# Attention and a gated two-matrix layer on one core: five warm-up products, a gate written over its own input in PSUM, its low part of two chunks by minus the identity, offsets in the planned order of the first chunks, and the weight checks moved to the last part

## The chip, the cores and the metric

The kernel runs on one core of one Trainium2 chip. The metric is device time in microseconds (us); lower is better. Engines are named as in the profile: PE (TensorE matmul), PEld (its weight loads), DVE (VectorE), ACT (ScalarE), POOL (GpSimd) and SP (SyncE, which issues the transfers).

## The reference

Attention with a causal window of 128 keys and 4 sink keys over q, k, v of [4, 8, 768, 64]; its output, as x of [3072, 512], goes through two matrices with a gate between them:

```python
keep = is_sink | in_window
scores = np.where(keep, scores, -1000000000.0)
a = np.exp(scores - np.max(scores, axis=-1, keepdims=True))
a = a / (np.sum(a, axis=-1, keepdims=True) + 1e-09)
x = (a @ v) ... reshape(3072, 512)
h = x @ w_in            # w_in [512, 2048]
g = h * np.cos(h)
return (g @ w_out).astype(np.float32)   # w_out [2048, 512]
```

## The kernel before

The 3072 rows are 12 chunks of 256 rows (two row blocks of 128). Chunks 0 to 2 are the first 256 rows of three batches. A chunk passes through 8 slots; a slot is 256 of the 2048 inner columns, so there are 96 slots, numbered 0 to 95.

**One slot**, built by `dense` (L562). Float32 accuracy comes from splitting every factor into a rounded high part and the rest, with three products for each product.
- `h_mm` (L399): 24 products of 256 columns on PE into the PSUM tile `h`, of one bank.
- `turns` (L408, ACT) writes `yt` from `h`; `rest` (L414, DVE) writes `r` in SBUF from `h` and `yt`; `cosine` (L421, ACT) works on `r` in place.
- `gate` (L426, DVE) multiplies `h` by `r` into `r`. With it `h` has been read for the last time and its bank is free.
- `g_hi` (L432, ACT) rounds `r` to `ghi`; `g_lo` (L438, DVE or POOL) writes `glo` = `r` - `ghi`.
- `out_mm` (L447): 12 products of 512 columns on PE from `ghi`, `glo` and w_out into `acc`, one PSUM bank for each row block.

Two `ghi` and two `glo` tiles exist (`GHI`, `GLO`), so `ghi` of slot m waits for the last product of slot m-2. The banks of `h` rotate: two for chunks 0 and 1, three from chunk 2 on; `h` of slot m+3 there takes the bank of slot m. After slot 7 of a chunk `out_copy` (L388) brings `acc` into a raw buffer and `out_store` (L463, SP) stores it.

**Weights** arrive as 32 pieces of 512 KB with two words a value. `load` (L492, SP) fills one of two raw buffers, three DVE instructions (L500, L506, L512) put the value together in `wt`, `round_hi` (L533, ACT) makes the high part and `rest_lo` (L536, DVE or POOL) the low part. All 32 go through chunk 0's time. **Checks**: `check_piece` (L543) loads each piece once more into a raw buffer (L556, SP), and DVE reduces it to one column of `tiny` (L551). At the end `tiny` is reduced to `tmin` (L1250, DVE), turned by one product (L1252, PE), reduced (L1253) and compared (L1254) into `redo`, which each engine loads (L1383) to branch (L1384) over the general path. The raw buffers are shared by weights, checks and output copies.

**The order of the work** on every engine is fixed while the kernel is built: `Plan.order` takes steps by a priority (a planned time) as their inputs come ready in its model, with the constants in `C`. One check goes to each slot from chunk 2 on (`if a > 1`), so the checks fill chunks 2 to 5, and the reduction L1250 is reached in chunk 6. `FILL` is a number of idle products (L1195) that PE may take early; `WARM` is the number of products (L251) ahead of the product `both` (L270), from which DVE gets the mask's limits (`neg` L275, masks L277 to L285).

## Time and profile before

| | us |
|---|---|
| median of 3 runs | 776.79 (775.74 to 777.22) |
| the profiled execution | 777.87 |
| its span, first to last instruction | 776.1 |
| busy: PE, DVE, ACT, POOL | 753.7, 611.7, 575.2, 151.5 |
| mean granted TensorE clock | 0.990 |

The sum of a forecast is made against the profiled execution, 777.87, and then set against the median, 1.08 lower. PE is busy for 97% of the span, so a change is read from what PE waits for, stretch by stretch, and from what stands ahead of the first and behind the last product. The stretches used below run from one chunk's output stores to the next.

### The profile page before, as it was taken

How to read it: one execution, taken by the hardware profiler on the slowest of the kernel's cores; microseconds unless marked ns; L12 is line 12 of the kernel's file. 1: busy time of each engine (PE TensorE's matmuls, PEld its weight loads, DVE VectorE, ACT ScalarE, POOL GpSimd, SP SyncE). 2: the span in 40 equal slices, each digit the busy share in tenths (PEclk: the TensorE clock that was granted, in tenths of full speed). 3: DMA queues.
4: the chain of work that ended last, by engine and by line, in shares of the span. 5: the costliest groups of instructions: out<-in, count | busy, mean ns of one | idle time of the engine just before them, and what ended most of it. 6: DMA issues, size and time to landing. Idle time of an engine off the chain costs nothing.

```text
span 776.1 us, 15387 instructions
## 1 busy us (share of the span) xinstructions
PE 753.7 (97%) x5029; PEld 666.3 (86%) x5029; DVE 611.7 (79%) x1607; ACT 575.2 (74%) x1337; POOL 151.5 (20%) x233
## 2 busy tenths in 40 slices
PE   8999879999999999999999999999999999999996
PEld 7677658888988999888989999999999999999994
DVE  6778878877878988989879988888878987964432
ACT  2768685779887787787886887897798788784332
POOL 1112101120313432122224221210211221220000
PEclk9999989999999999999999999999999999999998
DMA  5564464423265375375366352232242233110000
GB/s 157 142 177 131 142 175 143 109 56 53 47 179 121 57 185 138 67 190 140 64 158 177 58 114 53 43 74 41 40 87 51 50 71 61 30 40 3 28 1 32
DMA packets 215390, 71.51 MB, mean 92 GB/s; under 512 B 204036, under 2 KB 204036, under 8 KB 215300
## 3 DMA queue, kind: packets, MB, share of 16 engines
q1 hardware_dynamic: 215300, 70.43, 38.2%
q8 instruction: 42, 0.69, 0.4%
q14 instruction: 48, 0.39, 0.2%
HBM read 64.09 MB, written 6.29 MB: 91 GB/s over the span
## 4 chain that ended last, share of the span: by engine, by line
PE 79%; DVE 9%; DMA 5%; ACT 3%; issue 2%; SPq 1%; POOL 0%; DVEq 0%; ACTq 0%; POOLq 0%
PE h L399 30%; PE acc L447 29%; PE av L967 4%; PE tp L913 4%; PE s L811 4%; PE s L755 3%; PE av L943 2%; DMA raw<-in_moe_w_in_dram 2%; PE idle L1195 2%; DMA xk<-in_k_dram 1%; DVE glo L438 1%; DVE wt L551 1%; DVE plo L929 1%; DVE r L414 1%; DVE p L824 1%
## 5 line engine op out<-in xcount | busy, mean ns | idle before, releaser
L399 PE MATMUL h<-xhi,whi_in 128*128 128x256 f32 x768 | 223.3, 291 | 0.2 <-DVE r L426 0.2
L399 PE MATMUL h<-xlo,whi_in 128*128 128x256 f32 x768 | 217.0, 283 | 0.0
L399 PE MATMUL h<-xhi,wlo_in 128*128 128x256 f32 x768 | 216.7, 282 | 0.0
L447 PE MATMUL acc<-whi_out,ghi 128*128 128x512 f32 x384 | 158.0, 411 | 3.6 <-ACT whi_out L533 3.6
L399 PEld LDWEIGHTS h<-xhi,whi_in 128*128 128x128 f32 x768 | 145.6, 190 | 12.3 <-issue 2.7
L399 PEld LDWEIGHTS h<-xhi,wlo_in 128*128 128x128 f32 x768 | 145.9, 190 | 7.6
L447 PE MATMUL acc<-wlo_out,ghi 128*128 128x512 f32 x384 | 152.3, 397 | 0.0
L447 PE MATMUL acc<-whi_out,glo 128*128 128x512 f32 x384 | 151.5, 395 | 0.0
L399 PEld LDWEIGHTS h<-xlo,whi_in 128*128 128x128 f32 x768 | 145.8, 190 | 0.1
L824 DVE CUSTOM_DVE_ANT_0 p<-s,mk 128x264 f32<-128x264 f32 (+1 forms) x192 | 76.9, 401 | 35.1 <-PE s L811 22.6
L833 ACT ACTIVATE p<-p,st 128x264 f32<-128x264 f32 (+1 forms) x192 | 93.4, 488 | 0.7
L421 ACT ACTIVATE r<-r,neg 128x512 f32<-128x512 f32 x96 | 69.0, 724 | 27.5 <-DVE r L414 25.2
L447 PEld LDWEIGHTS acc<-whi_out,glo 128*128 128x128 f32 x384 | 72.6, 189 | 16.7
L432 ACT CAST ghi<-r 128x512 fp32r<-128x512 f32 x96 | 59.1, 616 | 31.8 <-PE acc L447 30.8
L438 DVE TENSOR_TENSOR glo<-r,ghi 128x512 fp32r<-128x512 f32 x80 | 57.2, 715 | 30.3 <-ACT ghi L432 29.6
L447 PEld LDWEIGHTS acc<-whi_out,ghi 128*128 128x128 f32 x384 | 73.1, 190 | 8.9 <-ACT whi_out L533 3.9
L447 PEld LDWEIGHTS acc<-wlo_out,ghi 128*128 128x128 f32 x384 | 73.4, 191 | 4.4 <-DVE wlo_out L536 0.4
L426 DVE TENSOR_TENSOR r<-h,r 128x512 f32<-128x512 f32 x96 | 65.3, 682 | 10.6 <-ACT r L421 10.2
L414 DVE SCALAR_TENSOR_TENSOR r<-h,yt 128x512 f32<-128x512 f32 x96 | 65.6, 683 | 6.1 <-ACT yt L408 3.7
L408 ACT ACTIVATE yt<-h 128x512 int32<-128x512 f32 x96 | 57.2, 596 | 14.9 <-PE h L399 13.0
L866 POOL TENSOR_TENSOR vr<-v,vr 128x192 fp32r<-128x192 f32 (+1 forms) x59 | 35.0, 593 | 159.1 <-ACT vr L861 140.9
L811 PE MATMUL s<-r,l 128*128 128x264 f32 (+2 forms) x288 | 61.0, 291 | 3.2 <-DVE r L802 1.7
(132 smaller groups left out, 1382.7 us busy)
## 6 DMA issues: line engine op xcount, KB each, us to landing
raw<-in_moe_w_in_dram SPq DMA_DIRECT2D x32, 512.0 KB
raw<-in_moe_w_out_dram SPq DMA_DIRECT2D x32, 512.0 KB
xk<-in_k_dram SPq DMA_DIRECT2D x256, 48.0 KB
out_dram<-raw SPq DMA_DIRECT2D x24, 256.0 KB
v<-in_v_dram SPq DMA_DIRECT2D x64, 96.0 KB
xq<-in_q_dram SPq DMA_DIRECT2D x144, 32.0 KB
v<-in_v_dram SPq DMA_DIRECT2D x32, 64.0 KB
xq<-in_q_dram SPq DMA_DIRECT2D x24, 64.0 KB
```

Source lines behind the costliest of these rows:

```text
L399: nc.tensor.matmul(out=o.h[:, t, :], lhsT=w[:, c, fs], rhs=xx[:, c, :], start=(c == 0 and n == 0), stop=(c == NC - 1 and n == 2),)
L408: nc.scalar.activation(out=yt, in_=o.h, func=AF.Copy, scale=INV2PI, bias=0.25)
L414: nc.vector.scalar_tensor_tensor(out=o.r, in0=o.h, scalar=INV2PI, in1=yt, op0=ALU.mult, op1=ALU.subtract)
L421: nc.scalar.activation(out=o.r, in_=o.r, func=AF.Sin, scale=TWOPI_DOWN, bias=quarter)
L426: nc.vector.tensor_tensor(out=o.r, in0=o.h, in1=o.r, op=ALU.mult)
L432: nc.scalar.copy(out=o.ghi, in_=o.r)
L438: e.tensor_tensor(out=o.glo, in0=o.r, in1=f32(o.ghi), op=ALU.subtract)
L447: nc.tensor.matmul(out=x.acc[j], lhsT=gg[:, t, j * P : (j + 1) * P], rhs=w[:, f, :], start=(f == 0 and n == 0), stop=(f == NFT - 1 and n = ...
L811: nc.tensor.matmul(out=o.s_ps[j][:, :w], lhsT=o.l[:, j * P : (j + 1) * P], rhs=r.rearrange("p n s -> p (n s)")[:, c0 : c0 + w], start=(n = ...
L824: nc.vector.tensor_tensor_reduce(out=o.p[:, j, :w], in0=o.s_ps[j][:, :w], in1=masks[min(o.i0 + j, 2)][:, :w], op0=ALU.add, op1=ALU.min, sc ...
L833: nc.scalar.activation(out=o.p[:, j, :w], in_=o.p[:, j, :w], func=AF.Exp, bias=o.lead.st[:, 0, o.nth, j : j + 1], scale=-1.0, accum_out=o. ...
L866: e.tensor_tensor(out=o.vr[:, :, 1, :], in0=o.v32, in1=f32(o.vr)[:, :, 0, :], op=ALU.subtract)
```

## The change

`WARM` goes from 11 to 5 and `FILL` from 100 to 68. The gate is written over `h` in PSUM. `ghi` is rounded from `h`, and `glo` is `h` - `ghi`, on DVE alone. In chunks 0 and 1 (`GM` = 2, 16 slots) a product of minus the identity with `ghi` adds -`ghi` to `h`, and ACT or DVE copies the rest to `glo`. `h` is now freed by `glo` and no longer by the gate, and it is begun and ended as one accumulation for the bank. The other constants of `C` are retuned, and `FIRST` holds offsets to the planned times of chunks 0 to 2. Checks are spread by a rule on the slots left: 19 stand in chunks 6 to 10 and 13 in the last chunk.

```diff
 C = {
-    ... "FILL": 100, ... "WARM": 11, ...
+    ... "CR": 1.618, "CS": 0.48, ... "FILL": 68, ... "GM": 2, ... "WARM": 5, ...
 }
+FIRST = {
+    "A": [7.43, 0.93, 2.38], "H": [0.45, -15.92, 4.04], "L": [-4.97, 5.1, 45.76], "M": [1.52, 2.74, 2.39],
+    "Q": [-7.6, -1.04, 10.09], "S": [-1.48, 6.81, 1.33], "V": [15.27, 1.57, 8.4], "W": [0.0, 0.59, 1.67],
+    "X": [12.35, 1.06, -9.48],
+}
...
-                        start=(c == 0 and n == 0), stop=(c == NC - 1 and n == 2),
+                        start=(t == 0 and c == 0 and n == 0), stop=(t == FG - 1 and c == NC - 1 and n == 2), skip_group_check=True,
...
-            nc.vector.tensor_tensor(out=o.r, in0=o.h, in1=o.r, op=ALU.mult)
+            nc.vector.tensor_tensor(out=o.h, in0=o.h, in1=o.r, op=ALU.mult)
...
-            nc.scalar.copy(out=o.ghi, in_=o.r)
+            nc.scalar.copy(out=o.ghi, in_=o.h)
...
-            e.tensor_tensor(out=o.glo, in0=o.r, in1=f32(o.ghi), op=ALU.subtract)
+            e.tensor_tensor(out=o.glo, in0=o.h, in1=f32(o.ghi), op=ALU.subtract)
+    def g_minus(o):
+        def fn(e):
+            nc.tensor.matmul(out=o.h, lhsT=minus, rhs=o.ghi, start=False, stop=True, skip_group_check=True)
+    def g_rest(o):
+        def fn(e):
+            o.glo = mp.tile([P, FG, NT], F32R, name=f"glo_{o.m}", tag="glo", bufs=C["GLO"])
+            copy(e, o.glo, o.h)
...
-            bh.users += [a0, a2, a4]
-            a6 = add(sub(FG * NT), g_lo(o), [a5, blo], t + C["DM"] + 10.8, port=True)
+            users = [a0, a2, a4, a5]
+            if plan.minus and a < C["GM"]:
+                m = add([("PE", 0.23)], g_minus(o), [a5], tm + 10.5)
+                c = [("ACT", act(FG * NT, False)), ("DVE", dve(FG * NT))]
+                a6 = add(c, g_rest(o), [m, blo], tm + 10.8)
+                users.append(m)
+            else:
+                a6 = add([("DVE", dve(FG * NT))], g_lo(o), [a5, blo], tm + 10.8)
+            bh.users += users + [a6]
...
-            if a > 1 and len(checked) < len(checks):
+            left = len(slots) - nh
+            while len(checked) < len(checks) - C["CR"] * min(left, NSLOT) - C["CS"] * max(left - NSLOT, 0):
                 checked.append(check_piece(plan, t + C["CK"], len(checked), checks[len(checked)][2]))
```

Three places show what that does to the order. **SP, its last transfers** (`raw` are the two raw buffers, `out_dram` the output). Before:

```order
L463 DMA out_dram<-raw_70 128x512
L704 DMA v_0_76<-in_v_dram 128x3x64
L463 DMA out_dram<-raw_71 128x512
L704 DMA v_1_77<-in_v_dram 128x3x64
L463 DMA out_dram<-raw_70 128x512
L463 DMA out_dram<-raw_71 128x512
L463 DMA out_dram<-raw_70 128x512
L463 DMA out_dram<-raw_71 128x512
```

With the change:

```order
L485 DMA out_dram<-raw_71 128x512
L485 DMA out_dram<-raw_70 128x512
L578 DMA raw_71<-in_moe_w_out_dram 128x1024
L578 DMA raw_70<-in_moe_w_out_dram 128x1024
...
L485 DMA out_dram<-raw_71 128x512
L485 DMA out_dram<-raw_70 128x512
L578 DMA raw_71<-in_moe_w_out_dram 128x1024
L1414 UNCONDITIONAL_BRANCH x2
L1417 TENSOR_LOAD redo
```

Twelve loads of checks (two are shown) now stand between the stores of chunk 10 and those of the last chunk, and a 32nd stands behind the last store, in the buffer that the first of the two stores reads.

**DVE, its last instructions** (slots 94 and 95; `L573 ISA` are the checks, each with a second instruction that writes its column). Before:

```order
L414 SCALAR_TENSOR_TENSOR r_95_9993<-h_95_9938,yt_81 128x512
L426 TENSOR_TENSOR r_95_9993<-h_95_9938,r_95_9993 128x512
L438 TENSOR_TENSOR glo_94_10011<-r_94_9951,ghi_94_10006 128x512
L438 TENSOR_TENSOR glo_95_10027<-r_95_9993,ghi_95_10022 128x512
L1253 TENSOR_REDUCE tmin_10052<-tp_10054 1x1
L1254 TENSOR_SCALAR redo_89<-tmin_10052 1x1
```

With the change:

```order
L437 TENSOR_TENSOR h_95_9909<-h_95_9909,r_95_9967 128x512
L449 TENSOR_TENSOR glo_94_9985<-h_94_9858,ghi_94_9978 128x512
L573 ISA wt1_73,tiny_88<-raw1_71 128x512
L573 ISA tiny_88 128x1
L449 TENSOR_TENSOR glo_95_10002<-h_95_9909,ghi_95_9997 128x512
L573 ISA wt0_72,tiny_88<-raw0_70 128x512
L573 ISA tiny_88 128x1
L573 ISA wt1_73,tiny_88<-raw1_71 128x512
L573 ISA tiny_88 128x1
L1284 TENSOR_REDUCE tmin_10030<-tiny_88 128x1
L1287 TENSOR_REDUCE tmin_10030<-tp_10032 1x1
L1288 TENSOR_SCALAR redo_89<-tmin_10030 1x1
```

The 30th check stands ahead of the last `glo`, the 31st and 32nd behind it, and the reduction to `tmin` behind all of them.

**PE, between the last product of slot 80 and the first of `h` of slot 85**, which takes the bank of slot 82. Before:

```order
4038 L447 MATMUL acc_80_1_9326<-whi_out_92,glo_80_9223 128x512
4039 L399 MATMUL h_84_9299<-xhi_10_8309,whi_in_90 128x256
4040 L399 MATMUL h_84_9299<-xhi_10_8309,wlo_in_91 128x256
4041 L399 MATMUL h_84_9299<-xlo_10_8319,whi_in_90 128x256
...
4045 L913 MATMUL tp_3_4_4_9357<-ident_79,p_3_4_4_8918 128x128 x4
4046 L399 MATMUL h_85_9369<-xhi_10_8309,whi_in_90 128x256
```

With the change:

```order
4036 L469 MATMUL acc_80_1_9252<-whi_out_92,glo_80_9070 128x512
4037 L410 MATMUL h_84_9232<-xhi_10_8294,whi_in_90 128x256
...
4043 L469 MATMUL acc_80_0_9209<-whi_out_92,ghi_81_9204 128x512
4044 L469 MATMUL acc_80_0_9209<-wlo_out_93,ghi_81_9204 128x512
4045 L469 MATMUL acc_80_0_9209<-whi_out_92,glo_81_9217 128x512
4046 L410 MATMUL h_84_9232<-xhi_10_8294,whi_in_90 128x256
...
4054 L469 MATMUL acc_80_1_9252<-whi_out_92,glo_81_9217 128x512
4055 L410 MATMUL h_85_9309<-xhi_10_8294,whi_in_90 128x256
```

Before, six products of `h` and four turns stand between the two; now twelve products of `h` and six of `acc` do.

## Rows read from the trace of the kernel before

**Rows 1.** The table by stretch of the whole core: start and end of the stretch in us, its length, then busy us (and instructions) of PE, PEld, DVE, ACT and POOL, the granted TensorE clock, the busy share of the DMA engines, and GB/s. From 214.20 on the stretches run from store to store.
```profile
81.80:85.20 3.40, 3.40 (x14) 2.98 (x15) 3.37 (x8) 2.49 (x7) 1.68 (x1) 0.50 0.12 48
105.70:112.50 6.80, 4.70 (x10) 3.43 (x11) 4.95 (x10) 5.20 (x17) 0.96 (x1) 0.50 0.77 200
214.20:274.80 60.60, 59.06 (x416) 53.87 (x416) 50.69 (x135) 49.29 (x111) 19.05 (x26) 1.00 0.50 118
274.80:335.30 60.50, 59.70 (x420) 54.20 (x419) 55.26 (x148) 48.14 (x115) 16.10 (x25) 1.00 0.52 126
335.30:394.50 59.20, 58.06 (x408) 52.86 (x407) 52.56 (x141) 47.76 (x115) 14.60 (x24) 1.00 0.55 132
394.50:456.10 61.60, 60.04 (x427) 55.11 (x426) 53.93 (x148) 49.13 (x116) 19.87 (x28) 1.00 0.52 126
456.10:514.20 58.10, 58.10 (x415) 53.57 (x414) 50.16 (x136) 49.06 (x115) 11.29 (x21) 1.00 0.34 67
514.20:569.40 55.20, 55.20 (x389) 50.93 (x388) 44.31 (x124) 44.95 (x113) 9.03 (x14) 1.00 0.30 56
569.40:626.10 56.70, 56.70 (x400) 52.23 (x399) 50.11 (x133) 48.58 (x111) 10.67 (x20) 1.00 0.32 61
626.10:684.50 58.40, 58.40 (x418) 53.98 (x417) 49.45 (x132) 47.79 (x113) 12.88 (x22) 1.00 0.24 49
```

**Rows 2.** The timeline of the last microseconds: start us, us, engine, line, operation, tiles, and in brackets the idle time before it and what ended it.
```profile
763.42 0.69 DVE L438 TENSOR_TENSOR glo<-r,ghi 128x512 fp32r<-128x512 f32 x1 [2.03 <-ACT ghi L432]
...
767.69 1.69 SPq L463 DMA_DIRECT2D out_dram<-raw  x2
...
768.01 0.39 PE L447 MATMUL acc<-whi_out,glo 128*128 128x512 f32 x1
...
768.24 0.27 PE L1252 MATMUL tp<-ident,tmin 128*1 128x128 f32 x1
...
768.86 0.14 DVE L1254 TENSOR_SCALAR redo<-tmin 1x1 int32<-1x1 f32 x1
```

**Rows 3.** The instructions of the lines that load `redo` (L1383) and branch on it (L1384), on SP's queue: shortest, median and longest duration in ns, and the start in us of the first and the last.
```profile
L1383 SPq TENSOR_LOAD <-redo x1: 729/729/729, 769.7 to 769.7; - x1
...
L1384 SPq COMPARE_BRANCH  x1: 45/45/45, 770.5 to 770.5; - x1
...
L1384 SPq EVENT_SEMAPHORE  x8: 17/17/17, 773.9 to 774.4; - x8
```

**Rows 4.** Timelines of SP and DVE at three checks, and of the reduction behind the last of them.
```profile
335.31 0.89 SPq L463 DMA_DIRECT2D out_dram<-raw  x2
...
337.55 0.34 SPq L556 DMA_DIRECT2D raw<-in_moe_w_in_dram  x1
...
366.82 0.43 SPq L556 DMA_DIRECT2D raw<-in_moe_w_out_dram  x1
...
370.71 0.69 DVE L551 CUSTOM_DVE_ANT_0 wt<-raw 128x512 f32<-128x512 f32 x1
...
397.56 0.38 SPq L556 DMA_DIRECT2D raw<-in_moe_w_out_dram  x1
...
403.46 0.69 DVE L551 CUSTOM_DVE_ANT_0 wt<-raw 128x512 f32<-128x512 f32 x1 [2.55 <-DMA raw<-in_moe_w_out_dram]
...
463.85 0.18 DVE L1250 TENSOR_REDUCE tmin<-tiny 128x1 f32<-128x32 f32 x1
```

**Rows 5.** The timeline of the first microseconds.
```profile
1.36 5.06 PE L251 MATMUL warm<-ident 128*128 128x128 f32 x22 [1.36 <-POOL ident L238]
...
3.40 0.94 SPq L492 DMA_DIRECT2D raw<-in_moe_w_in_dram  x2
...
6.93 0.16 DVE L275 COPY neg<-both 128x2 f32<-128x2 f32 x1 [3.40 <-PE both L270]
...
7.70 1.07 PE L1195 MATMUL idle<-gt 128*128 128x256 f32 x7
...
9.57 0.77 DVE L500 TENSOR_SCALAR wt<-raw 128x512 int32<-128x512 int32 x2 [0.24 <-DVE mk L285]
```

**Rows 6.** The instructions of the low part `glo` (L438, on DVE and on POOL): count, shortest, median and longest duration in ns, start of the first and the last in us.
```profile
L438 DVE TENSOR_TENSOR glo<-r,ghi x80: 640/691/1550, 65.2 to 763.4; 128x512 fp32r<-128x512 f32 x80
...
L438 POOL TENSOR_TENSOR glo<-r,ghi x16: 1280/1297/1682, 65.6 to 691.0; 128x512 fp32r<-128x512 f32 x16
```

**Rows 7.** The chain of waits in order of time, two pieces of it: start us, us, what.
```profile
711.71 1.43 PE h L399 x12
...
757.49 10.92 PE acc L447 x48
```

**Rows 8.** The timeline around two weight pieces: one in chunk 0, and the last.
```profile
107.80 0.80 PE L447 MATMUL acc<-whi_out,ghi 128*128 128x512 f32 x1 [3.63 <-ACT whi_out L533]
...
148.52 0.65 DVE L536 TENSOR_TENSOR wlo_out<-wt,whi_out 128x512 fp32r<-128x512 f32 x1
...
150.24 0.40 PE L447 MATMUL acc<-whi_out,ghi 128*128 128x512 f32 x1
```

**Rows 9.** The timeline around the low part of slot 82: the last product of slot 80, then `ghi` and `glo` of slot 82.
```profile
689.69 0.39 PE L447 MATMUL acc<-whi_out,glo 128*128 128x512 f32 x1
...
690.28 0.60 ACT L432 CAST ghi<-r 128x512 fp32r<-128x512 f32 x1
...
690.96 1.29 POOL L438 TENSOR_TENSOR glo<-r,ghi 128x512 fp32r<-128x512 f32 x1 [0.95 <-ACT ghi L432]
```

More of the change, by code (lines that the diff above doesn't have):

```diff
@@ L54, in __init__ @@
         self.steps, self.bufs, self.port, self.ahead = [], {}, set(), set()
+        self.minus = False
     def buf(self, tag, n):
@@ L319, in attn_moe_kernel, with extra @@
         pass
+    def extra(kind, a):
+        return FIRST[kind][a] if a < 3 else 0.0
     env = Rec()
@@ L580, in dense @@
                     mm.append(
-                        add([("PE", 0.655)], h_mm(o, x, tt, half), d + mm[-1:], t + C["DH"] + (3.5, 5.8)[tt] + 0.6 * half)
+                        add([("PE", 0.655)], h_mm(o, x, tt, half), d + mm[-1:], t + C["DH"] + extra("H", a) + (3.5, 5.8)[tt] + 0.6 * half)
                     )
@@ L584, in dense @@
             x.blo.users += mm
-            a0 = add([("ACT", act(FG * NT, False))], turns(o), mm + [by], t + C["DM"] + 7.2)
-            a2 = add([("DVE", dve(FG * NT))], rest(o), [a0, br], t + C["DM"] + 8.0)
+            tm = t + C["DM"] + extra("M", a)
+            a0 = add([("ACT", act(FG * NT, False))], turns(o), mm + [by], tm + 7.2)
+            a2 = add([("DVE", dve(FG * NT))], rest(o), [a0, br], tm + 8.0)
             by.users.append(a2)
-            a3 = add([("ACT", act(FG * NT) + 0.09)], cosine(o), [a2], t + C["DM"] + 8.9, table="sin")
-            a4 = add([("DVE", dve(FG * NT))], gate(o), [a3], t + C["DM"] + 9.5)
-            bh.users += [a0, a2, a4]
-            a5 = add([("ACT", act(FG * NT))], g_hi(o), [a4, bhi], t + C["DM"] + 10.2)
-            a6 = add(sub(FG * NT), g_lo(o), [a5, blo], t + C["DM"] + 10.8, port=True)
-            br.users += [a5, a6]
+            a3 = add([("ACT", act(FG * NT) + 0.09)], cosine(o), [a2], tm + 8.9, table="sin")
+            a4 = add([("DVE", dve(FG * NT))], gate(o), [a3], tm + 9.5)
+            br.users.append(a4)
+            a5 = add([("ACT", act(FG * NT, False))], g_hi(o), [a4, bhi], tm + 10.2)
+            users = [a0, a2, a4, a5]
+            if plan.minus and a < C["GM"]:
+                m = add([("PE", 0.23)], g_minus(o), [a5], tm + 10.5)
+                bhi.users.append(m)
+                env.minus.users.append(m)
+                c = [("ACT", act(FG * NT, False)), ("DVE", dve(FG * NT))]
[4 more added lines that the diff above has]
+            bh.users += users + [a6]
             for tt in range(FG):
@@ L597, in dense @@
                     late = 2.6 * j if a == len(chunks) - 1 and s >= NSLOT - 2 else 0.3 * j
-                    i = add([("PE", 0.655)], out_mm(o, x, tt, j), d, t + C["LAG"] * T + (0.0, 1.95)[tt] + late)
+                    i = add([("PE", 0.655)], out_mm(o, x, tt, j), d, t + C["LAG"] * T + extra("L", a) + (0.0, 1.95)[tt] + late)
                     bhi.users.append(i)
@@ L621, in banded_path @@
         plan = Plan()
+        plan.minus = True
         add, buf = plan.add, plan.buf
@@ L1005, in before_softmax @@
             nonlocal first, vs_last
-            t = head_time(g)
+            t, dq, ds = head_time(g), C["DQ"] + extra("Q", o.a), C["DS"] + extra("S", o.a)
             if o.i0 == CB and o.h == 0:
@@ L1161, in after_softmax @@
             bav = buf("av", 1)
-            p0 = add([("PE", 0.107 * o.n)], turn(o), o.nm + [pt], t + C["DA"] + 1.3)
+            p0 = add([("PE", 0.107 * o.n)], turn(o), o.nm + [pt], t + da + 1.3)
             o.bp.users.append(p0)
-            p1 = add([("ACT", act(o.n * P, False))], p_hi(o), [p0, bhi], t + C["DA"] + 1.8)
-            p2 = add([("DVE", dve(o.n * P))], p_lo(o), [p1, blo], t + C["DA"] + 2.3)
+            p1 = add([("ACT", act(o.n * P, False))], p_hi(o), [p0, bhi], t + da + 1.8)
+            p2 = add([("DVE", dve(o.n * P))], p_lo(o), [p1, blo], t + da + 2.3)
             pt.users += [p1, p2]
@@ L1177, in after_softmax @@
             bxb = buf("xb", 1)
-            y1 = add([("ACT", act(NT, False))], x_low(o), [y0, bxb], t + C["DA"] + 4.8)
+            y1 = add([("ACT", act(NT, False))], x_low(o), [y0, bxb], t + da + 4.8)
             if o.odd == 0:
                 x.bf = buf("x", 1)
-            y2 = add([("DVE", dve(NT))], x_sum(o, x), [y0, y1] + (x.sums[o.pair] or [x.bf]), t + C["DA"] + 5.1)
+            y2 = add([("DVE", dve(NT))], x_sum(o, x), [y0, y1] + (x.sums[o.pair] or [x.bf]), t + da + 5.1)
             bav.users += [y1, y2]
@@ L1185, in after_softmax @@
             if o.odd:
-                x.bf.users += split_x(plan, x, o.a, o.pair, t + C["DA"] + 5.4)
+                x.bf.users += split_x(plan, x, o.a, o.pair, t + da + 5.4)
         idle = buf("b1", 1)
```

79 lines of the change are left out of this document (41 added, 38 removed).

## The prediction

> **What bounds the kernel now.** I read the table by stretch first, then the two ends of the timeline, then the places where two kinds of work meet. The table [rows 1] shows PE busy through whole chunks: from 456.10 to 684.50 its busy time equals the stretch, 58.10 of 58.10 and so on. So from chunk 6 on only fewer or shorter products, or a wait that PE does not have now, change the time. The four stretches before, 214.20 to 456.10, hold 31 of the 32 checks, and there PE is idle for 1.54, 0.80, 1.14 and 1.56 us, 5.0 in all. Ahead of that PE waits for weights and is slowed: in 81.80 to 85.20 and 105.70 to 112.50 the granted clock is 0.50, the lower of its two levels (1.2 against 2.4 GHz), with 3.40 + 4.70 = 8.1 us of busy time in them, and the products of `acc` at 107.80 had waited 3.63 us for a weight's high part [rows 8]. The last weight's low part ends at 148.52 + 0.65 = 149.17, and 1.1 us later PE begins the products that need it [rows 8]. So the head is set by the stream of weights through DVE, the middle by PE alone. The tail starts when the last product does, at 768.01; `redo` is ready at 769.00 [rows 2], SP loads it at 769.7, when its last store is issued, branches at 770.5, goes on at 773.9 [rows 3], and the span ends at 776.1.
>
> **The sum is made against the profiled execution, 777.87 us; the median of the runs, 776.79, lies 1.08 lower.** A measurement of this kernel can tell about 0.2%, 1.55 us, from no change.
>
> **Start: -1.4.** The 11 warm-ups are 22 passes in 5.06 us, 0.23 each [rows 5], so six fewer end 2.76 us earlier. With them go the limits (`neg` at 6.93) and the masks, which DVE finishes just before it takes the first weights at 9.57. Those were issued at 3.40 and, as the idle time of 0.24 us behind a mask shows, were there by then. The gain is between 0, if the weights themselves are the limit, and 2.7. I take the middle, since the masks, the first heads and the first weights all have to come earlier for the rest to move. The 32 idle products dropped (`FILL`) were taken where PE had nothing else, and cost nothing either way.
>
> **Weights and chunk 0: -0.5.** In the changed order DVE has 6.3 us less work ahead of the last weight piece: four low parts of `glo` at 0.69 [rows 6], 2.8, three gates, rests or weights' low parts at 0.65 [rows 8], 2.0, and small work of 1.5. If DVE is the limit there, the last weight is ready 6.3 us earlier. But PE has then done less: 36 products of `h` that stood ahead of chunk 0's last `acc` now stand behind it. Twelve take 1.43 us, 0.119 each [rows 7], so 4.3 us are still to do. Of the 16 products by minus the identity, seven also come later; nothing like them is in the trace, and a product of 512 columns in the `acc` chain takes 10.92 / 48 = 0.23 us [rows 7], which I take: 1.6. Together -6.3 + 5.9 = -0.4, with rounding -0.5. The other nine of these products and the copies behind them fall into time in which PE waits. The bounds are -6.4 (all of DVE's gain, the displaced products fall into later gaps) and +2 (DVE is not the limit: nothing is gained, and the nine products cost 2.1).
>
> **Low parts off POOL: 0.** POOL's 16 take 1.30 us each [rows 6] and are gone; DVE or ACT does 0.69 instead. From chunk 2 on neither is the limit in the quiet stretches: DVE is busy 50 of 58 us there [rows 1]. If that cover went, DVE's extra would come to a few tenths a chunk.
>
> **Checks moved: -2.2.** By busy time the checks cost PE 5.0 us. By pace, the same products take (58.10 + 55.20 + 56.70 + 58.40) / 1622 = 0.141 us in the quiet stretches and 0.145 before [rows 1], which makes 6.6 over 1671 products, part of it another mix. I take 5.6, or 0.18 for each of the 31. In the changed order 19 stand in chunks 6 to 10, in groups of three or four behind each pair of stores: 19 x 0.18 = 3.4. Nothing shows what grouping does. It could be free (-5.6 in all), or cost what is saved (0).
>
> **Bank of `h` held longer: +1.0.** `h` of slot m+3 now waits for `glo` of slot m, which waits for `ghi`, which waits for the end of slot m-2's products. At slot 82 that took from 690.08 (the end of the product at 689.69) to 692.25, 2.2 us, with POOL's 1.29; with DVE's 0.69 it is 1.6 [rows 9]. In the changed order six products of `acc` and twelve of `h` lie between at the place shown, 6 x 0.23 + 1.43 = 2.8 us, against 1.3 before (six of `h`, four turns). So the retuned order has made the room, and the wait should be hidden as a rule. Where DVE has a check or a transposition ahead of `glo` it comes 0.7 later and some of it shows: I allow 1.0, with bounds of 0 and 7 (0.1 for about 70 slots).
>
> **Last chunk, the checks beside the last products: +0.5.** Twelve checks run from the stores of chunk 10 to the end. With two raw buffers a pair takes about one load and one DVE pass, and a load alone takes up to 370.71 - 366.82 = 3.9 us and, crowded, 403.46 - 397.56 = 5.9 [rows 4]. From about 735 the 30th check, now ahead of the last `glo`, is then done about 765. Before, that `glo` began at 763.42 [rows 2], and the last slot's 12 of the chain's 48 products begin 12 x 0.23 ahead of its end, at 765.7 [rows 7]. A small delay, at most 3.
>
> **The last check: +5.8.** Its load stands behind the last stores on SP, into the buffer that the first of them reads. That store was issued at 767.69 [rows 2]; the buffer is free when it has landed, and in the quiet pair 335.31 to 337.55 that took 2.24 [rows 4]: 769.93. The load takes up to 3.89: 773.82. The check takes 0.69, the reduction to `tmin` 0.18 [rows 4], the turn and the compare 769.00 - 768.24 = 0.76 as now [rows 2]: `redo` at 775.45. SP loads it then, where it did at 769.7 [rows 3]: 5.8 later, and what follows it (branch, 6.4 us to the end) is the same. Nothing else lies beside it; this is bare time. Bounds: 5.0 with a faster load, 7.8 with the crowded 5.9.
>
> **Sum:** -1.4 - 0.5 - 2.2 + 1.0 + 0.5 + 5.8 = +3.2, so 781.1 for a profiled execution and **780.0** for the median.
>
> **Rivals.**
> - *R1, faster: the head gives back far more.* If weights come early enough that PE is fed around 81 and 107 us, the two stretches at half clock run at full (8.1 / 2 = 4.05) and the wait of 3.63 goes: 7.7 on top, 773.4 profiled, **772.3**. For it: DVE's work there falls, and the offsets touch only chunks 0 to 2, where PE's waits lie. Against it: what PE has to do behind the last weight grows by almost as much. It decides when the head gives over 3.2 us more than my terms.
> - *R2, no change:* the same at half the size, 3.2 of the 7.7, cancels the tail: **about 776.8**.
> - *R3, a cold start:* the seven idle products behind the warm-ups take 0.15 us each for 256 columns, where each warm pass of 128 took 0.23 [rows 5]: PE was slow at first and fast after 11 warm-ups. If five no longer bring the upper level, the first real products run at half the clock for as long as the warm-ups took, and 5.06 us of work takes twice as long: **785.1**. Against it: the idle products between them remain, and this early PE mostly waits.
> - The Trainium skill, page "TensorE: Matmul & The Clock Gate", Part 1, says that the throttled clock is the default and that activity releases it. By that rule fewer warm-ups speak against this change, and the sum would be that of R3; the table agrees so far as its lower level stands where PE is idle for 2.10 of 6.80 us.
> - *R4, the bank binds:* if `glo` is late by 0.2 us in each of 80 slots, because DVE's queue holds it, 16 us: **796**. It decides when `glo` ends over 2.8 us after slot m-2's products; for slot 82 it was 2.2.
>
> **Chances.** Forecast 0.46, with a range of its own of 778.4 to 783.5 (start and checks down, tail up). R1 0.30, since all of PE's waits of the head lie in its reach. R2 0.12, R3 0.08, R4 0.04. Slower by over 0.2% are the forecast, R3 and R4, 0.58; R2 is within; R1 is faster. The range of 771 to 786.5 takes in R1 with the terms' bounds, the forecast and R3, and leaves out R4 and the far ends of R1 and R3.
>
> **What would show it.** The last chunk's products end, a load is issued on SP about 2.2 us behind the first store, and `redo` is ready about 7 us behind the last product instead of 1.0. PE is never idle in 214 to 456 as long as before, and has a few tenths of idle time in each of chunks 6 to 10. The last weight's low part ends before 146, with PE's clock still at 0.50 somewhere between 80 and 115. Products of `h` that wait for a `glo` are few. It would be wrong if the clock's row held no half stretch behind 20 us and PE's wait near 107 were gone (R1), if the first slices showed a lower clock than before (R3), if `h` waited for `glo` in most slots (R4), or if the end stood about 8 us behind the last product as now, which would mean that the last check lies beside something that I have missed.

## The result and the profile after

The change makes the kernel slower by 0.6%: a ratio of 1.0063 (1.0047 to 1.0078) over 13 executions of each, 780.66 us against 775.59. The forecast was 780.0 with slower at 0.58. One execution of the change took 1046.51 us at a mean granted clock of 0.652 and is left out of the ratio and of the spread given here; without it the change's median is 780.36. Both kernels spread more than the first three runs of before told (before 773.7 to 777.5, the change 777.8 to 785.4), and the 776.79 that the sum was set against lies 1.2 above the median of 13. So by its ratio the change costs 4.9 us (3.6 to 6.0) where the sum said 3.2, just below that interval.

The profiled execution of the change took 779.71 us, 1.84 more than that of before, and divides like this. The extra time of a product is what lies between its start and the next beyond the usual spacing of its kind, worked out from all starts. What is taken for usual shifts the totals of these rows by several us, and the differences between the two kernels by about 1.

| part | term of the sum | measured |
|---|---|---|
| chunk 0's products end | -7.7 (start -1.4, DVE -6.3) | -8.5 (153.4 to 144.9) |
| PE work left behind chunk 0, at usual spacing | +5.9 | +6.2 (581.7 to 587.9) |
| extra time in chunks 1 to 10 (checks, bank) | -1.2 (-2.2 and +1.0) | -2.4 (32.6 to 30.2) |
| extra time in the last chunk, to the last product | +0.5 | +0.9 |
| last product's start to the end | +5.8 | +5.8 (8.09 to 13.90) |
| sum | +3.2 | +2.0 (1.8 by the spans) |

**The table by stretch of the change**, with the columns of [rows 1]: three stretches of the head, then from store to store, chunks 2 to 9.

```profile
20.00:81.80 61.80, 58.58 (x330) 41.34 (x330) 51.47 (x142) 50.75 (x143) 14.34 (x12) 1.00 0.61 169
81.80:112.50 30.70, 28.98 (x164) 21.70 (x164) 27.10 (x64) 28.14 (x68) 1.33 (x2) 1.00 0.62 172
...
208.71:269.63 60.92, 60.92 (x438) 56.41 (x437) 48.13 (x130) 51.89 (x120) 13.30 (x22) 1.00 0.30 58
269.63:325.36 55.73, 55.70 (x389) 50.77 (x388) 47.04 (x129) 48.57 (x109) 11.46 (x18) 1.00 0.31 58
325.36:382.95 57.59, 57.59 (x415) 53.47 (x414) 47.44 (x130) 51.33 (x117) 13.61 (x24) 1.00 0.32 61
382.95:441.05 58.10, 58.10 (x413) 53.57 (x412) 47.69 (x128) 49.04 (x112) 13.83 (x26) 1.00 0.33 62
441.05:502.32 61.27, 61.27 (x441) 56.76 (x440) 52.92 (x145) 52.08 (x126) 15.69 (x26) 1.00 0.43 94
502.32:558.08 55.76, 55.19 (x386) 50.56 (x385) 44.20 (x122) 48.74 (x111) 10.89 (x18) 1.00 0.37 87
558.08:619.68 61.60, 60.40 (x414) 54.37 (x414) 53.77 (x143) 52.49 (x125) 15.75 (x25) 1.00 0.44 88
619.68:677.00 57.32, 56.97 (x402) 51.92 (x401) 47.29 (x133) 48.66 (x113) 11.07 (x17) 1.00 0.39 88
```

PE's idle time has moved with the checks: 5.0 us in chunks 2 to 5 before [rows 1], 0.03 now; none in chunks 6 to 9 before, 2.1 now (0.57 + 1.20 + 0.35 in the last three). In this execution the two half-clock stretches of [rows 1] are gone, and between 81.8 and 112.5 PE executes 164 products, where 123 fitted before.

The held bank has a line of its own in the list of who waited for whom (us in total, times, longest):

```profile
PE h L410 <- DVE glo L449: 1.7, 4, 0.6
```

From chunk 2 on, `h` waits 1.7 us for a `glo` in all; the kernel before has no such wait. The sum had put +1.0 for it.

**The timeline at the last weight and at chunk 0's end**, and the low parts grouped as in [rows 6]; the weights' low part is L558 now, `acc` L469, `glo` L449.

```profile
138.80 0.68 DVE L558 TENSOR_TENSOR wlo_out<-wt,whi_out 128x512 fp32r<-128x512 f32 x1
...
144.52 0.39 PE L469 MATMUL acc<-whi_out,glo 128*128 128x512 f32 x1
```

```profile
L449 DVE TENSOR_TENSOR glo<-h,ghi x80: 651/684/694, 205.2 to 760.2; 128x512 fp32r<-128x512 f32 x80
```

The last weight is ready at 139.5, 9.7 us earlier than in [rows 8], and the wait of 3.63 us for a weight's high part is gone. `glo` from PSUM and SBUF takes 0.68 us, where from SBUF it took 0.69 [rows 6].

**The timeline of the first microseconds** (answers to [rows 5]; `s` are the first scores, L1228 the idle products, `whi_in` the high part of the second weight piece):

```profile
4.41 0.16 DVE L283 COPY neg<-both 128x2 f32<-128x2 f32 x1 [0.88 <-PE both L278]
...
5.83 2.05 PE L1228 MATMUL idle<-gt 128*128 128x256 f32 x8
...
7.81 1.65 PE L788 MATMUL s<-tk,tq 64*128 64x128 f32 x4
7.91 0.43 DVE L522 TENSOR_SCALAR wt<-raw 128x512 int32<-128x512 int32 x1 [0.74 <-DMA raw<-in_moe_w_in_dram]
9.27 0.43 DVE L522 TENSOR_SCALAR wt<-raw 128x512 int32<-128x512 int32 x1 [0.94 <-DMA raw<-in_moe_w_in_dram]
...
14.99 0.42 DVE L401 COPY tq<-qk 128x256 f32<-128x256 f32 x1 [2.12 <-PE qk L764]
...
17.55 0.61 ACT L555 CAST whi_in<-wt 128x512 fp32r<-128x512 f32 x1
```

The same high part in the kernel before:

```profile
14.07 0.61 ACT L533 CAST whi_in<-wt 128x512 fp32r<-128x512 f32 x1
```

The limits come 2.5 us earlier, but DVE then waits 0.74 and 0.94 us for the weights' transfers, and 2.12 us for a product `qk` of PE, which is slow here (the run with eleven warm-ups below shows by how much). The high part of the second weight piece begins at 17.55, where it began at 14.07 before.

**The tail of the change**, a timeline as in [rows 2], then SP's load of `redo` as in [rows 3]:

```profile
763.68 1.70 SPq L485 DMA_DIRECT2D out_dram<-raw  x2
...
764.00 0.39 PE L469 MATMUL acc<-whi_out,glo 128*128 128x512 f32 x1
...
765.77 0.34 SPq L578 DMA_DIRECT2D raw<-in_moe_w_out_dram  x1
769.45 0.69 DVE L573 CUSTOM_DVE_ANT_0 wt<-raw 128x512 f32<-128x512 f32 x1 [6.77 <-DMA raw<-in_moe_w_out_dram]
...
770.42 0.37 PE L1286 MATMUL tp<-ident,tmin 128*1 128x128 f32 x1 [6.03 <-DVE tmin L1284]
...
771.14 0.14 DVE L1288 TENSOR_SCALAR redo<-tmin 1x1 int32<-1x1 f32 x1
```

```profile
L1417 SPq TENSOR_LOAD <-redo x1: 451/451/451, 771.4 to 771.4; - x1
```

The load is issued 2.09 us behind the first store (2.24 in the sum), lands within 3.68 (up to 3.89), and `redo` is ready 7.28 us behind the start of the last product, where it was 0.99 [rows 2]. DVE's 6.77 us of idle time "<-DMA raw" and PE's 6.03 "<-DVE tmin" are one wait seen from two engines: this is what bare time at the end looks like.

### The profile page after: what moved, and what is told of

Read it like the earlier page. It is cut to its first block, busy times and chain, and to the rows that moved or that the text cites. A ratio compares the mean times of both kernels' runs of the same rounds, so it can differ in the third digit from the quotient of the medians.

```text
span 777.9 us, 15317 instructions
## 1 busy us (share of the span) xinstructions
PE 754.3 (97%) x5001; PEld 664.2 (85%) x5001; DVE 597.3 (77%) x1584; ACT 599.3 (77%) x1377; POOL 143.7 (18%) x230
## 4 chain that ended last, share of the span: by engine, by line
PE 78%; DVE 7%; DMA 6%; ACT 5%; issue 2%; SPq 1%; POOL 0%; DVEq 0%; POOLq 0%; ACTq 0%
PE h L410 29%; PE acc L469 27%; PE av L1000 4%; PE tp L946 4%; PE s L844 4%; DMA raw<-in_moe_w_out_dram 3%; PE s L788 2%; PE av L976 2%; DMA raw<-in_moe_w_in_dram 2%; PE idle L1228 2%; DMA xk<-in_k_dram 1%; ACT p L866 1%; PE qk L764 1%; DVE p L857 1%; PE gp L928 1%
## 5 line engine op out<-in xcount | busy, mean ns | idle before, releaser
L469 PE MATMUL acc<-whi_out,ghi 128*128 128x512 f32 x384 | 156.0, 406 | 0.0
L469 PE MATMUL acc<-wlo_out,ghi 128*128 128x512 f32 x384 | 151.4, 394 | 0.0
L469 PE MATMUL acc<-whi_out,glo 128*128 128x512 f32 x384 | 150.5, 392 | 0.0
L469 PEld LDWEIGHTS acc<-whi_out,glo 128*128 128x128 f32 x384 | 72.1, 188 | 16.5
L437 DVE TENSOR_TENSOR h<-h,r 128x512 f32<-128x512 f32 x96 | 66.2, 691 | 17.2 <-ACT r L432 16.8
L469 PEld LDWEIGHTS acc<-whi_out,ghi 128*128 128x128 f32 x384 | 72.5, 189 | 5.8 <-ACT raw L399 0.5
L469 PEld LDWEIGHTS acc<-wlo_out,ghi 128*128 128x128 f32 x384 | 72.8, 190 | 4.6
L443 ACT CAST ghi<-h 128x512 fp32r<-128x512 f32 x96 | 55.7, 580 | 22.0 <-PE acc L469 18.0
L449 DVE TENSOR_TENSOR glo<-h,ghi 128x512 fp32r<-128x512 f32 x80 | 54.6, 683 | 18.3 <-ACT ghi L443 17.5
L886 POOL TENSOR_SCALAR p<-p,st 128x264 f32<-128x264 f32 (+2 forms) x70 | 35.9, 528 | 164.0 <-DVE st L876 108.4
```

The costliest lines, as they stand in the source:

```text
L437: nc.vector.tensor_tensor(out=o.h, in0=o.h, in1=o.r, op=ALU.mult)
L443: nc.scalar.copy(out=o.ghi, in_=o.h)
L449: e.tensor_tensor(out=o.glo, in0=o.h, in1=f32(o.ghi), op=ALU.subtract)
L469: nc.tensor.matmul(out=x.acc[j], lhsT=gg[:, t, j * P : (j + 1) * P], rhs=w[:, f, :], start=(f == 0 and n == 0), stop=(f == NFT - 1 and n = ...
L886: e.tensor_scalar(out=o.p[:, j, :w], in0=o.p[:, j, :w], scalar1=r, scalar2=1.0, op0=ALU.mult, op1=ALU.mult)
```

## The experiments

Twelve runs, each timed against the kernel before on the same chip; medians in us. The change ran again beside the first ones tried on it.

### The last check

**In the change, the last check ahead of the last stores**; all instructions of DVE and PE keep their order.

```diff
+            if left == 0:
+                some()      # the loop that adds the checks, ahead of the two output copies
             dense(plan, xs[a], a, s, ...)
-            while len(checked) < ...
+            some()
```

> The 32nd check takes its raw buffer ahead of the two output copies of the last chunk, so that its load stands ahead of the last stores on SP; all else is as in the change. Theory (the last check behind the last store is bare time, 5.8 us): redo is ready within 2.5 us of the last product and the time falls by 5.2 (4.5 to 5.8) to 775.5, the same as before within 0.2%. Rival (the end is set by the stores' landing and the branch, which the check only accompanies): less than 1.5 us, 779.5 or more.

Measured: 777.15 against 776.39 of before, 1.0008 (0.9983 to 1.0032), and 780.65 of the change beside it, so 3.5 us less. The timeline of its end:

```profile
765.80 2.72 SPq L485 DMA_DIRECT2D out_dram<-raw  x2
...
766.13 0.39 PE L469 MATMUL acc<-whi_out,glo 128*128 128x512 f32 x1
766.79 0.69 DVE L573 CUSTOM_DVE_ANT_0 wt<-raw 128x512 f32<-128x512 f32 x1 [2.11 <-DMA raw<-in_moe_w_out_dram]
...
768.39 0.14 DVE L1294 TENSOR_SCALAR redo<-tmin 1x1 int32<-1x1 f32 x1
```

`redo` is ready 2.4 us behind the last product's start, and the end 9.27 behind it (span 775.4) against 13.90: 4.6 less. The theory's mechanism holds and the rival's 779.5 is out of the interval. The size falls short: the median is 3.5 lower, below the 4.5 to 5.8 of the theory. Two things in the trace go that way: the last of 13 loads in a row still lands behind the products (DVE waits 2.11 us for it), and the last product itself starts 2.1 us later than in the profile of the change (766.13 against 764.00), with 3.2 us of `h` waiting for `glo` where there were 1.7.

**In the kernel before, the last check behind the last store:**

```diff
-            if a > 1 and len(checked) < len(checks):
+            if a > 1 and len(checked) < len(checks) - 1 or nh == len(slots):
```

> The kernel before with one edit: the 32nd check is taken from its slot and put behind the last output store. Theory (bare time at the end): 5.8 more (5.0 to 7.8), 1.0075 of before, with redo ready about 7 us behind the last product instead of 1.0. Rival (the stores' landing and the branch set the end whatever the check does): 1.5 more at most.

Measured: 781.84 against 776.35, 1.0069 (1.0050 to 1.0088), 5.4 us more. Its end:

```profile
765.54 0.39 PE L447 MATMUL acc<-whi_out,glo 128*128 128x512 f32 x1
...
767.30 0.34 SPq L556 DMA_DIRECT2D raw<-in_moe_w_out_dram  x1
770.80 0.69 DVE L551 CUSTOM_DVE_ANT_0 wt<-raw 128x512 f32<-128x512 f32 x1 [9.15 <-DMA raw<-in_moe_w_out_dram]
...
772.50 0.14 DVE L1254 TENSOR_SCALAR redo<-tmin 1x1 int32<-1x1 f32 x1
```

From the last product to the end (779.6) it takes 14.06 us, against 8.09. One check in the wrong place costs about as much as the whole change does; that is shown from both sides.

### The checks and the bank

**In the change, the checks by the rule of before:**

```diff
-            while len(checked) < len(checks) - C["CR"] * min(left, NSLOT) - C["CS"] * max(left - NSLOT, 0):
+            if a > 1 and len(checked) < len(checks):
```

> The changed kernel with the rule of before for the checks, one to each slot from chunk 2 on; constants and offsets as in the change. Theory (checks late save 2.2 in the middle, cost 0.5 in the last chunk and 5.8 behind it): 4.1 less, 776.6, with PE idle for some 1.2 us in each of chunks 2 to 5 and none in 6 to 10. Rival (groups of checks behind each pair of stores cost PE more than single ones): below 775, with chunks 6 to 10 shorter by over 1 us each and chunks 2 to 5 hardly longer.

Measured: 784.17, 1.0128 (1.0093 to 1.0164). I expected 4.1 less than the change and got 3.5 more, and the rival falls as well. Its chunks 2 to 5, store to store:

```profile
209.70:274.40 64.70, 62.44 (x436) 56.46 (x435) 52.49 (x145) 52.55 (x120) 12.24 (x20) 1.00 0.48 113
274.40:333.60 59.20, 56.64 (x384) 51.12 (x383) 51.26 (x133) 46.55 (x107) 14.59 (x24) 0.97 0.52 121
333.60:396.00 62.40, 60.70 (x427) 54.72 (x427) 55.36 (x152) 51.01 (x123) 11.21 (x19) 1.00 0.53 126
396.00:459.00 63.00, 60.39 (x423) 54.67 (x422) 54.80 (x152) 53.16 (x123) 13.40 (x23) 1.00 0.54 128
```

PE is idle for 9.1 us in them, against 5.0 in the kernel before with the same checks, and the extra time of all products there is 25.1 against 9.7 in the change, which has no check in these chunks: 15.4 for 31 checks, 0.50 each. The list of who waited for whom in 209.7 to 459, longest first (us in total, times, longest):

```profile
PE h L410 <- DVE glo L449: 4.5, 6, 1.6
```

The longest item is the bank: `h` waits for a `glo`. So in this kernel a check is dearer than the 0.18 of the sum, and taking the checks out of these chunks is worth more than the 2.2 that I put down for it. The two prices are not of one measure: by extra time, chunks 2 to 5 against the quiet ones, a check costs about 0.3 in the kernel before. Of the 15.4 us, 1.5 lie in a stretch at half clock, 286.9 to 290.3 (the 0.97 in the second row). And the order is planned anew here, with constants that were chosen for late checks. Two theories were left for why: the held bank (B), or the low parts that DVE has from POOL (C).

**In the kernel before, the gate over `h`, `glo` on DVE alone:**

```diff
-            nc.vector.tensor_tensor(out=o.r, in0=o.h, in1=o.r, op=ALU.mult)
+            nc.vector.tensor_tensor(out=o.h, in0=o.h, in1=o.r, op=ALU.mult)
...            (g_hi and g_lo read o.h)
-            bh.users += [a0, a2, a4]
+            br.users.append(a4)
-            a6 = add(sub(FG * NT), g_lo(o), ...
-            br.users += [a5, a6]
+            a6 = add([("DVE", dve(FG * NT))], g_lo(o), ...
+            bh.users += [a0, a2, a4, a5, a6]
```

> The kernel before with the gate written over h: ghi is rounded from h, glo is h - ghi on DVE alone, the bank of h is held until glo and r is free at the gate, and the plan is told so. Constants, warm-ups and the checks' places as before. The prediction's price for the held bank is 1.0 (0 to 7). Theory B (held banks make PE feel each check, 0.5 us where it was 0.18): chunks 2 to 5, with their 31 checks, lose 5 to 10 us more than the 17.9 of before, and the time is 5 to 10 more. Rival (r, which was held until glo and is now free at the gate, was as much of a limit): no more than 1.5 either way, in the chunks without checks 0.5 less each.

Measured: 786.35 against 776.96, 1.0118 (1.0096 to 1.0141), 9.2 more.

**In the kernel before, `glo` on DVE alone and nothing else:**

```diff
-            a6 = add(sub(FG * NT), g_lo(o), ...
+            a6 = add([("DVE", dve(FG * NT))], g_lo(o), ...
```

> The kernel before with one edit: glo is made on DVE alone (POOL made 16 of 96); the gate stays in r and the bank of h is free at the gate. It is the run with the gate over h without the gate over h. Theory B (that run's 9 us come from the bank that is held until glo): within 2 us of before, chunks 2 to 5 as before (17.9 us in which PE does not move in). Rival C (they come from the low parts that DVE has to take): 5 to 10 more, chunks 2 to 5 at 22 or more.

Measured: 779.98 against 776.63, 1.0044 (1.0021 to 1.0067), 3.4 more. The tables of both, chunks 2 to 5, the gate over `h` first:

```profile
212.42:276.68 64.26, 61.71 (x439) 56.28 (x438) 54.62 (x152) 50.60 (x120) 12.52 (x24) 1.00 0.50 113
276.68:337.91 61.23, 59.88 (x420) 54.19 (x419) 54.09 (x147) 47.58 (x112) 15.29 (x25) 1.00 0.55 126
337.91:396.12 58.21, 56.28 (x397) 51.58 (x395) 49.02 (x138) 46.76 (x113) 13.04 (x22) 1.00 0.53 129
396.12:462.88 66.76, 64.68 (x446) 58.70 (x445) 58.80 (x160) 50.98 (x125) 18.13 (x28) 0.97 0.53 123
```

```profile
212.01:273.21 61.20, 58.63 (x409) 52.82 (x409) 52.91 (x145) 48.22 (x114) 14.80 (x23) 1.00 0.52 119
273.21:332.92 59.71, 59.10 (x418) 53.97 (x418) 52.76 (x145) 48.75 (x116) 17.91 (x24) 1.00 0.58 132
332.92:395.43 62.51, 60.81 (x428) 55.00 (x427) 53.29 (x144) 49.77 (x121) 14.18 (x25) 1.00 0.51 123
395.43:454.56 59.13, 58.84 (x411) 53.19 (x410) 53.31 (x141) 47.30 (x111) 20.59 (x31) 1.00 0.56 133
```

PE is idle for 7.9 us with the gate over `h` and 5.2 with the low parts alone, against 5.0 [rows 1]; the extra time of all products in these chunks is 23.0, 19.2 and 17.9. So of the 9.2 us about 3.4 come with DVE's low parts, which the sum had at nothing, and about 6 with the gate over `h`. That the held bank takes these 6 is not shown. With the gate over `h`, the list of waits has no `h` that waited for a `glo` in chunks 2 to 5 (one of 0.8 us behind them), and in the whole run:

```profile
PE h L399 <- DVE glo L438: 1.8, 3, 0.8
```

The extra time in these chunks differs by 3.8 alone, and 1.5 of that lie in a stretch at half clock, 413.3 to 416.7 (the 0.97 in the last row of the first table). The order of all engines is planned anew in each of these kernels, and the plan knows that the bank is held, so the rest can be the order as well as the bank. Theory B's 5 to 10 is met for both together and its "within 2" for the low parts alone is not.

**In the change, the bank free at the gate** (from chunk 2 on the gate goes to `r` as before, and `r` is held until `glo`):

```diff
-            nc.vector.tensor_tensor(out=o.h, in0=o.h, in1=o.r, op=ALU.mult)
+            o.g = o.h if o.m < C["GM"] * NSLOT else o.r
+            nc.vector.tensor_tensor(out=o.g, in0=o.h, in1=o.r, op=ALU.mult)
...            (g_hi and g_lo read o.g; from chunk 2 on bh.users = [a0, a2, a4], br.users = [a5, a6])
```

> The changed kernel, but from chunk 2 on the gate is written to r in SBUF as before, so that the bank of h is free at the gate and no longer held until glo. Checks, constants and offsets as in the change. Theory A (the bank costs 1.0 in all): 1 less, 779.7. Theory B, formed on the run with the checks in their old places, where PE waited for glo: the held bank makes PE feel each check, so chunks 6 to 9, which hold 15 checks, lose 2 to 4 us together of the time that PE does not move in, and the run is 2 to 4 less. Rival C (DVE's extra low parts, which POOL had, are what PE feels): no gain, since these stay on DVE.

Measured: 787.05 against 776.35, 1.0132 (1.0091 to 1.0173), 6.4 more than the change. Theories A and B fail; C's "no gain" holds, but says nothing of a loss. With the gate in `r`, of which there are two, `rest` of slot m+2 waits for `glo` of slot m. The constants of the change were chosen for the gate over `h`, and the extra time rises in chunks 5 to 7 above all (13.7 against 8.5). Whether the two `r` or the order that no longer suits costs the 6.4 stays open: no run has a third `r`. What it shows is that a bank that is free at the gate does not by itself bring time back. The gate over `h` lends the bank of `h` longer and gives `r` back earlier.

### The head

**The change once more:**

> The changed kernel as it is, beside the others on the same chip. Both theories: 780.7 us, 1.006 of the kernel before. Its first 13 runs spread over 777.8 to 785.4 where those of before spread over 3.8 us, so a second profile is wanted: if the spread comes from the head, the end of chunk 0's products moves against 144.9 us while the time from there to the last product (619.3) stays; if it comes from the tail, the time from the last product to the end moves against 13.6.

Measured: 780.65 against 776.39, 1.0055 (1.0029 to 1.0081). The profiled one was the slowest of its 12, at 789.13, and differs from the first profile of the change in the head above all: chunk 0's products end at 153.4 instead of 144.9, and from there to the end of the last product it takes 620.1 us instead of 619.5. Its head in the table by stretch:

```profile
20.00:81.80 61.80, 57.05 (x282) 39.09 (x280) 44.62 (x125) 44.38 (x124) 14.00 (x12) 0.86 0.56 153
```

The same stretch holds 282 products where the other execution had 330, at a mean granted clock of 0.86: it is at 0.50 from 33.9 to 40.7 and from 71.4 to 81.6 us, with PE busy throughout. Of the 11 other executions, 776.5 to 787.3 us at mean clocks of 0.995 to 0.984, time and clock go together (correlation -0.89, 8 us for 0.01). In the first 12 of the change they do so less (-0.61, 3 us for 0.01): at clocks of 0.994 and 0.995 these took 777.8 to 784.0. So the head's clock is one source of the spread; that it is the only one is not shown.

**Eleven warm-ups in the change** (`"WARM": 5` to 11; DVE and ACT keep their order, PE's shifts by six products):

> The changed kernel with 11 warm-up products instead of 5. Theory (six warm-ups delay the limits, the masks and with them the first weights): 1.4 more (0 to 2.7), 782.1, with the limits at 6.9 and the first weight's shift at about 9.6 instead of 7.9. Rival (the clock's start is what matters, and five warm-ups leave it low): faster than the change by 1 to 5 us, with the products ahead of 10 us shorter.

Measured: 779.67, 1.0040 (1.0018 to 1.0062), within the noise of the change's 780.65. The 1.4 us of the sum are not in the time, and the cost of R3 is not either. The trace shows why, in the first products, at the second weight piece and in the head:

```profile
7.75 1.20 PE L1228 MATMUL idle<-gt 128*128 128x256 f32 x8
9.21 0.92 PE L788 MATMUL s<-tk,tq 64*128 64x128 f32 x4 [0.27 <-ACT tk L399]
...
15.04 0.60 ACT L555 CAST whi_in<-wt 128x512 fp32r<-128x512 f32 x1
```

```profile
20.00:81.80 61.80, 57.83 (x300) 39.69 (x299) 45.61 (x130) 47.24 (x136) 14.43 (x12) 0.92 0.56 155
```

With 11 warm-ups eight idle products take 1.20 us and four score passes 0.92; with 5 they take 2.05 and 1.65. So R3's mechanism exists: behind 5 warm-ups PE is slow to about 17 us, for eight idle products at 16.46 still take 1.71 us and four score passes at 18.09 take 0.92. And it costs what the early limits bring. With 5, DVE begins the first weight piece at 7.91 instead of 9.62, then waits for the second transfer and for the slow `qk`, and the high part of the second piece begins at 17.55 instead of 15.04, the fourth low part ends at 28.5 instead of 25.6. Behind that the two profiles cannot be compared: the one with 11 has its clock at 0.50 from 31.0 to 37.8 and from 68.5 to 71.9 (0.92 over the stretch shown), the one with 5 has not, and after eight pieces the kernel with 11 is 0.9 behind (47.7, 46.8). Leaving out six warm-ups starts the work 2.5 us earlier, and the slow PE has taken that back before 18 us.

**A hundred idle products in the change** (`"FILL": 68` to 100):

> The changed kernel with 100 idle products as before, not 68. In the change they ran out by 26 us, in the kernel before by 58. The prediction's price is 0. Rival (they keep PE busy in the gaps of the head, and without them the granted clock falls there in some executions: 0.50 for 9 us near 36 and 12 us near 76 in one profile of the change, none in another): mean clock 0.992 or more in nearly all executions, spread under 5 us, median 1 to 3 less.

Measured: 792.02 against 776.35, 1.0206 (1.0182 to 1.0230), 11.7 more than the change by the two ratios. Both the price of 0 and the rival fail. The edit does more than add 32 products: in the plan they take PE's time, and from early in chunk 0 on, PE and DVE have another order. Chunk 0's products end at 156.3, the last weight's low part at 151.0. The spread is 5.2 us at clocks of 0.979 to 0.991, so idle products until 51 us do not steady the clock. What of the 11.7 is the idle products' own time and what the other order, this run can't tell.

**No products by minus the identity** (`"GM": 2` to 0):

> The changed kernel without the products by minus the identity (GM 0): in chunks 0 and 1 too glo is h - ghi on DVE. 16 products of 0.23 less on PE, 12 copies less on ACT and 12 more passes of 0.69, 8.3 us, on DVE. Theory (DVE sets the stream of weights in chunk 0, so its work there counts): the last weight comes later by some 3 to 4 us, the end of chunk 0 by 2 to 4; 1 to 3 more in all. Rival (PE sets chunk 0 once weights are early): 16 x 0.23 = 3.7 less on PE, 1 to 3 less in all.

Measured: 780.32, 1.0053 (1.0029 to 1.0077): the same as the change. Chunk 0's products end at 147.2, 2.3 later than in the change, and the PE work left behind it, 584.8, is 3.1 less. The two cancel, as both the theory's later weight (141.5 against 139.5) and the rival's shorter work are there; part of what is later can be the clock, which in this execution is 0.89 over 60 to 70 us and 0.94 over 70 to 80. In the change each of these products lasts as long as one of `acc` (0.39 us), and behind 13 of the 16 the next product starts 0.23 to 0.34 us later, where the sum took 0.23 from [rows 7]:

```profile
L454 PE MATMUL h<-ghi,gt x16: 392/397/502, 66.1 to 193.1; 128*128 128x512 f32 x16
```

**No offsets** (`FIRST` all zero):

> The changed kernel with all offsets of FIRST at zero; all else as in the change. In its trace the last weight's low part ended at 139.5 us where it was 149.2 before, and 6.2 us of PE work moved behind chunk 0. Theory (the offsets bring the weights ahead of other DVE work and move PE's work back): the last low part ends 4 to 10 later, less PE work is left behind chunk 0, and the two cancel to within 2 us in the time. Rival (the offsets bring the net gain of the head, 8.5 - 6.2 = 2.3 and more): 2 to 6 more.

Measured: 790.15, 1.0164 (1.0124 to 1.0203), 8.5 more than the change by the two ratios; the rival's direction, beyond its size. The last weight is ready at 145.9 instead of 139.5 and chunk 0's products end at 153.4, while the work behind chunk 0 is only 2.5 less. The theory's cancelling, which the sum relies on, fails here. How far that is the order is open. This execution has its clock at 0.50 from 35.6 to 42.4 and from 62.9 to 69.7 us, and the second profile of the change, with two such falls and all its offsets, ended chunk 0 at 153.4 too. Its six executions have mean clocks of 0.973 to 0.990, those of the change 0.978 to 0.995. And 2.3 us of it stand behind the load of `redo`, from which to the end it takes 8.8 us here and 6.5 in the change.

### A better version

**The last check ahead, and 12 checks in the last chunk** (the edit of the first run, and `"CR": 1.618` to 1.5):

> A better version by the experiments: the changed kernel with the last check ahead of the last stores, as in the run that tried that, and with 12 checks in the last chunk instead of 13 (CR 1.5). In that run the 13 loads took 2.3 us each and the last check still ended 1.3 us behind the last product. Theory: one load less, redo within 1 us of the last product's end and the end 7.9 behind it: 1 to 2 less than that run's 777.15, 775 to 776, at least as fast as before. Rival (the check ahead of the last chunk costs what it saves): 777.

Measured: 775.76 against 776.96, 0.9983 (0.9962 to 1.0004). Its end:

```profile
761.57 0.69 DVE L573 CUSTOM_DVE_ANT_0 wt<-raw 128x512 f32<-128x512 f32 x1 [1.14 <-DMA raw<-in_moe_w_out_dram]
...
763.38 0.39 PE L469 MATMUL acc<-whi_out,glo 128*128 128x512 f32 x1
...
764.23 0.14 DVE L1294 TENSOR_SCALAR redo<-tmin 1x1 int32<-1x1 f32 x1
```

The last check is done before the products are, and the end (771.5) stands 8.12 us behind the last product, as before. This is the lowest median of all changed kernels. Its interval against the kernel before takes in 1, so it is not shown to be faster than that one (whose medians in these sessions are 775.59 to 776.96).

## Why the prediction was right, point by point

**The tail decided it, and its term was right to a tenth:** +5.8 forecast, +5.8 in the trace, 5.4 when one check alone was moved in the kernel before, and 4.6 to 5.8 back, between last product and end, in the two runs that took it ahead. The load was issued 2.09 us behind the store and landed within 3.68, so the mechanism is the one forecast; that the sum meets it to a tenth is luck, since the time from the load of `redo` to the end, which was taken as fixed, is 6.0 to 8.8 us in the 14 profiles.

**The head was right as a balance, and its first term in part by luck.** DVE has less to do ahead of the last weight, and PE keeps what it did not do: -7.7 and +5.9 forecast, -8.5 and +6.2 in the trace. What moved is what was read from the order: 36 products of `h` and seven by minus the identity stand behind chunk 0. The gain was not won as forecast. The prediction took it from the start and from DVE's work and expected the clock at 0.50 somewhere between 80 and 115. In the profiled execution that stretch is gone and so is the wait of 3.63 us, which is the sign that the prediction names for R1. By R1's own count these are 7.7 of the 8.5. R1's time did not come, because they are part of the 8.5 and not on top of it, and because the work moved back takes 6.2 of it. And the size changes from one execution to the next: in the second profile of the change, whose clock fell near 37 and 76, chunk 0 ended at 153.4, as in the kernel before. With no offsets or with 100 idle products the time is 8 to 12 us longer, from the order, the clock or both.

**Four prices were wrong, and hid each other or did not matter.**
- *Start, -1.4:* nothing shows in the time. DVE waits 0.74 and 0.94 us for the weights' transfers, the other bound that the prediction names. Then the mechanism of R3, which the prediction gave a chance of 0.08, takes the rest: PE stays slow to about 17 us, and the high part of the second weight piece begins 3.5 us later than in the kernel before. R3's price of 5.06 us is not there: with 11 warm-ups the median is the same within the noise.
- *Checks -2.2 and bank +1.0:* together -1.2 forecast, -2.4 measured. `h` waits 1.7 us for a `glo` in the change, so the bank's term is of the right order there, and what the checks gave back is more than 2.2. With the checks in their old places, the kernel with the change's constants has 4.5 us of that wait in chunks 2 to 5, and a check costs 0.45 to 0.50 us there. "DVE has a check ahead of `glo` and some of it shows" was the mechanism; I sized it at 1.0 from the cover at one slot (2.8 us against 2.2 [rows 9]). What the gate over `h` costs in the kernel before, some 6 us, is not traced to the bank.
- *Low parts off POOL, 0:* 3.4 in the kernel before. The cover that I named, DVE's idle time in the quiet chunks, does not hold there: with `glo` on DVE alone PE is idle for 1.3 us in chunks 6 to 9, where it was never idle, and for 5.2 against 5.0 in chunks 2 to 5.
- *Idle products, "cost nothing either way":* they enter the plan, and 32 more make another order, 11.7 us slower.

**The median:** the sum gave +3.2, the profiles differ by 1.8 and the medians of 13 by 5.1. Of the 3.2 us between, 2.3 are that the profiled execution of before stood that far above its median, and 0.9 that the one of the change stood below its own. The head's clock is the likely reason, which the prediction named for R1 and did not count: the profiled execution of the change had none of the falls that its second profile had. That is argued and not shown.

## What to carry to other kernels

Look first at what stands behind the last product: a transfer and a check that nothing covers are paid in full, and the same work a few us earlier is free. A buffer that is released later is paid where other work on the releasing engine delays that release: with the checks among them, `h` waited 4.5 us in four chunks, with the checks moved 1.7 in ten, so price the pair. A profile is one execution: where the clock falls in some executions and not in others, take two before the size of a term is believed. In a statically planned order even filler changes the plan, so the order has to be read again for each constant.
